# Attention's first batch in two passes over its tiles of queries, with loads and operands in two portions

## The chip, the cores and the metric

The kernel runs on one core of a Trainium2 chip. The metric is the device time of one execution in microseconds (us), the median of several runs. Five engines work side by side, each on its own queue of instructions in program order: TensorE (PE, the matrix engine), VectorE (DVE), ScalarE (ACT), GpSimd (POOL) and SyncE (SP, which here only issues transfers).

## The reference

Attention over 4 batches of 8 heads, 576 positions and head size 64, with a causal mask and a bias from a running sum of gates, feeds a dense mixture of 8 experts:

```python
scores = scale * np.matmul(q, k.transpose(0, 1, 3, 2))
cum = np.cumsum(np.maximum(s, 0.0), axis=-1)
bias = -(cum[:, :, :, None] - cum[:, :, None, :])
scores = np.where(causal, -1000000000.0, scores + np.minimum(bias, 0.0))
attn = softmax(scores)
x = np.matmul(attn, v)          # 2304 tokens of 512 features
P = x @ w_gate                  # exp, then 8 rounds of row and column scaling
out = sum(P[:, e:e+1] * (relu(x @ w1[e]) @ w2[e]) for e in range(8))
```

The expert layer cuts each expert's 1024 hidden features into 4 units of 256, so there are 32 units.

## The kernel before

**Attention.** The 8 heads of a batch are taken as 4 pairs (`g` counts pairs over all batches, 16 in all). A pair has 5 tiles of 128 queries (`i` = 0 to 4; the last has 64 queries of each head). Because of the causal mask, tile `i` has scores of (i + 1) x 128 columns. One slot of the loop is one tile of one pair, and the steps of a slot are staggered over four turns `ti` of the loop: `st0` makes the scores (tile `sc`), their row minimum (L366, into tile `T`) and the exponential; `st1` normalizes; `st2` transposes (tile `tr`, copied to `at` or `al`); `st3` multiplies with the values (tile `pv`) and writes the result, split in a high and a low part, to `xh` and `xl`.

**Operands of a head.** `load_head` fetches the transposed queries and keys of one head, each twice (to the lower and the upper 64 partitions), so 4 transfers of 144 KB a head. `prep_head` makes from them the operands `qa`, `qb`, `ka`, `kb`: high parts on VectorE, low parts on GpSimd (L329, L333; on VectorE for the first two heads), a copy of the high part by a transfer (`qb<-qa`, L327), and the rows of the gates' running sum by two or three small transfers (L314, L317). The raw tiles have two buffers, so the next head's queries and keys are fetched when GpSimd has read those of the head before.

**The expert layer beside attention.** Its first 4 units run on the first tokens while attention runs. `EARLY` lists, for each batch, blocks of tokens; for a block a unit needs `g1_half` (L104), `relu_parts` (L118 on ScalarE, L119 on VectorE) and `g2_chunk` (L137, L147, L149). These steps stand in a queue, `Stream`; `fill` takes steps from it in each turn. A batch's steps enter the queue when its attention is complete: at `ti` 22, 42 and 62 for batches 0 to 2, after attention for the last. A unit's weights are loaded (`w_load_early`) and split (`w_split_early`: L68 on ScalarE, L69 on GpSimd).

**What sets the order.** The program is recorded by these loops; a scheduler then fixes each engine's order before the launch. At run time every engine, and SP's queue of transfers, works strictly in that order and waits on semaphores. All of attention's loads but the first four are issued by SP.

Of the kernel before, what the change touches and what calls it, by code (L numbers as in the profile page):

```python
# [8 lines left out]
F32 = mybir.dt.float32  # L9
F32R = mybir.dt.float32r  # L10
AF = mybir.ActivationFunctionType
ALU = mybir.AluOpType
# [15 lines left out]
    [(0, 256), (256, 256)],  # L28
# [3 lines left out]
]  # L32
TP = 384
# [4 lines left out]
def fused_kernel(ctx: ExitStack, tc: tile.TileContext, qT, kT, v, s, w_gate, wu, out):  # L38
# [121 lines left out]
    class Stream:  # L160
# [4 lines left out]
        def add_visit(self, vi, load, split):  # L165
# [46 lines left out]
    with ExitStack() as actx:  # L212
# [9 lines left out]
        def load_head(h):  # L222
            tag, bufs = ("raw", 2) if h else ("T", 5)
            for which, src in (("q", qT), ("k", kT)):
                raw = apool.tile([P, S], F32, name=f"raw{which}", tag=tag, bufs=bufs)
                eng = nc.scalar if h < 2 and which == "k" else nc.sync
                eng.dma_start(out=raw[:D], in_=src[h])
                eng.dma_start(out=raw[D:], in_=src[h])
                raws[h, which] = raw
# [3 lines left out]
        load_head(0)  # L233
        load_head(1)
# [8 lines left out]
        crow_d = dram.tile([B * H, 6, S], F32, name="crow_d")  # L243
        cum = apool.tile([B * H, S], F32, name="cum", tag="T", bufs=5)
        cr = xl[: B * H, 2:4, :].rearrange("p k n -> p (k n)")
        cr = cr[:, : 6 * S].rearrange("p (r n) -> p r n", n=S)
        nc.gpsimd.memset(cr[:, 0:2, :].bitcast(F32), 1.0)
        nc.gpsimd.memset(cr[:, 4:6, :].bitcast(F32), -1.0)
# [6 lines left out]
        nc.scalar.copy(cr[:, 2, :], cum)  # L255
        gates_done = nc.vector.tensor_tensor(
            out=cr[:, 3, :], in0=cum, in1=cr[:, 2, :].bitcast(F32), op=ALU.subtract
# [25 lines left out]


        QW = S + D
        qas, qbs, vtt = [], [], []
        for n in range(4):
            qa = apool.tile([P, QW], F32R, name=f"qa{n}")
            qb = apool.tile([D + 4, QW], F32R, name=f"qb{n}")
            z = slice(S - D, S) if n % 2 else slice(S, QW)  # L290
            nc.gpsimd.memset(qa[:, z].bitcast(F32), 0.0)
            nc.gpsimd.memset(qb[:, z].bitcast(F32), 0.0)
            qas.append(qa)
            qbs.append(qb)

        for n in range(2):
            vt = apool.tile([P, 5, P], F32, name=f"vt{n}")
            nc.gpsimd.memset(vt[:D, 4, :], 0.0)
            vtt.append(vt)

        ops = {}

        def prep_head(h):
            rq, rk = raws.pop((h, "q")), raws.pop((h, "k"))
            ka = apool.tile([P, S], F32R, name="ka", tag="ka", bufs=4)
            kb = apool.tile([D + 4, S], F32R, name="kb", tag="kb", bufs=4)
            qa, qb = qas[h % 4], qbs[h % 4]
            if h < 2:
                rows = cr[h : h + 1].bitcast(F32)
            else:  # L310
                rows = crow_d[h : h + 1]
            at = [(0, 0, S)] if h % 2 == 0 else [(0, 0, S - D), (S - D, S, D)]
            for i, o, n in at:
                nc.sync.dma_start(  # L314
                    out=qb[D : D + 4, o : o + n].bitcast(F32), in_=rows[:, 2:6, i : i + n]
                )
            nc.sync.dma_start(out=kb[D : D + 4, :].bitcast(F32), in_=rows[:, 0:4, :])  # L317
            for i, o, n in at:
                nc.vector.tensor_scalar(  # L319
                    out=qa[:, o : o + n], in0=rq[:, i : i + n], scalar1=-1.0, scalar2=None,  # L320
# [634 lines left out]
```

## Time and profile before

| what | value |
|---|---|
| median of 3 runs | 1766.21 us (1765.97 to 1766.9) |
| the profiled execution, its own time | 1765.97 us |
| its span, first to last instruction | 1764.2 us (1.8 us lie outside it) |
| TensorE busy | 1724.8 us, 98% of the span |
| VectorE busy | 1185.0 us, 67% |
| ScalarE busy | 597.3 us, 34% |
| GpSimd busy | 461.2 us, 26% |
| mean granted TensorE clock | 0.995 of full speed |

A busy share is an average over the whole program. The first 90 us, attention of batch 0, look unlike the rest: there TensorE has gaps, and from about 95 us to 340 us it has nearly none.

### The profile page before, as it was taken

To read this page: it belongs to the slowest core of one execution; us is meant where nothing else is said; L and a number is where in the kernel's file an instruction comes from. 1 tells how busy PE (TensorE), PEld (TensorE's weight loads), DVE (VectorE), ACT (ScalarE), POOL (GpSimd) and SP (SyncE) were. 2 spreads that over 40 slices of the span, in tenths; PEclk is the share of its full clock that TensorE was granted. 3 is DMA by queue.
4 is the path that set the end of the run, shared out by engine and by line. 5 is a ranking of instruction groups with operands and counts; after the bars stand their busy time and mean duration, and the time that the engine had idled before them with its cause. 6 is when DMAs were issued, how large, how long until landed. Compare 5 with 4: busy or idle time off the path is not lost.

```text
span 1764.2 us, 26154 instructions
## 1 busy us (share of the span) xinstructions
PE 1724.8 (98%) x9629; PEld 1536.3 (87%) x9629; DVE 1185.0 (67%) x2394; ACT 597.3 (34%) x1419; POOL 461.2 (26%) x511
## 2 busy tenths in 40 slices
PE   5799999999999999999999999999999999999999
PEld 4688888878988888888888888888888888888887
DVE  6777676689666666666666666666666666666665
ACT  5776766543422222222222222222222222222221
POOL 4653443123221222221222222221222222222210
PEclk9899999999999999999999999999999999999999
DMA  6543433111000000000000000000000000000002
GB/s 169 160 142 91 126 90 96 44 36 55 13 24 24 14 25 25 25 25 24 25 25 19 24 19 25 25 25 20 17 25 25 25 25 25 25 25 18 23 2 108
DMA packets 44271, 77.26 MB, mean 44 GB/s; under 512 B 5936, under 2 KB 15152, under 8 KB 44112
## 3 DMA queue, kind: packets, MB, share of 16 engines
q1 hardware_dynamic: 43824, 75.00, 14.0%
q8 instruction: 76, 1.25, 0.3%
q10 hardware_dynamic: 320, 0.59, 0.1%
q14 instruction: 51, 0.42, 0.1%
HBM read 65.13 MB, written 5.16 MB: 40 GB/s over the span
## 4 chain that ended last, share of the span: by engine, by line
PE 92%; DVE 4%; DMA 2%; issue 1%; ACT 0%; SPq 0%; POOL 0%; DVEq 0%; POOLq 0%; ACTq 0%
PE g L137 44%; PE c L815 35%; PE g L104 5%; PE sc L357 3%; PE pv L460 2%; PE tr L430 2%; DVE xs L719 1%; DMA rawq<-qT 1%; DMA rawk<-kT 1%; PE g L483 0%; DVE acc L149 0%; DVE xel L719 0%; DVE T L366 0%; DVE hl L119 0%; DVE qa L319 0%
## 5 line engine op out<-in xcount | busy, mean ns | idle before, releaser
L137 PE MATMUL g<-w,hh 128*128 128x512 f32 x2304 | 711.6, 396 | 0.2 <-DVE acc L149 0.2
L153 DVE SCALAR_TENSOR_TENSOR acc<-g,prob,acc 128x512 f32<-128x512 f32 x504 | 377.1, 748 | 236.0 <-PE g L137 234.8
L137 PEld LDWEIGHTS g<-w,hh 128*128 128x128 f32 x2304 | 424.0, 188 | 64.1 <-issue 0.5
L137 PE MATMUL g<-w,hl 128*128 128x512 f32 x1152 | 442.2, 396 | 3.2 <-DVE hl L119 3.2
L118 ACT ACTIVATE hh<-tap 128x384 fp32r<-128x384 f32 x336 | 176.4, 526 | 680.2 <-DVE tap L828 356.2
L815 PE MATMUL c<-xh,wc 128*128 128x384 f32 x1344 | 398.9, 337 | 0.0
L828 DVE TENSOR_TENSOR tap<-c,tap 128x384 f32<-128x384 f32 x588 | 320.2, 557 | 52.9 <-PE c L815 31.8
L119 DVE SCALAR_TENSOR_TENSOR hl<-tap,hh 128x384 fp32r<-128x384 f32 x336 | 189.3, 564 | 170.5 <-ACT hh L118 160.4
L815 PE MATMUL c<-xeh,wc 128*128 128x384 f32 x1008 | 297.8, 335 | 0.0
L137 PEld LDWEIGHTS g<-w,hl 128*128 128x128 f32 x1152 | 216.3, 188 | 55.5 <-DVE hl L119 4.4
L815 PEld LDWEIGHTS c<-xh,wc 128*128 128x128 f32 x1344 | 247.8, 188 | 11.3
L815 PE MATMUL c<-xl,wc 128*128 128x384 f32 x672 | 226.8, 337 | 0.0
L69 POOL TENSOR_TENSOR wc<-r,wc 128x256 fp32r<-128x256 f32 x112 | 85.5, 764 | 465.5 <-ACT wc L68 465.5
L815 PEld LDWEIGHTS c<-xeh,wc 128*128 128x128 f32 x1008 | 187.1, 188 | 11.2
L69 POOL TENSOR_TENSOR w<-r,w 128x512 fp32r<-128x512 f32 x64 | 86.8, 1358 | 391.6 <-ACT w L68 387.9
L815 PE MATMUL c<-xel,wc 128*128 128x384 f32 x504 | 170.6, 338 | 0.0
L815 PEld LDWEIGHTS c<-xl,wc 128*128 128x128 f32 x672 | 125.9, 187 | 11.3
L104 PE MATMUL g<-xh,w 128*128 128x256 f32 (+1 forms) x512 | 115.8, 302 | 1.9 <-DVE hl L119 1.0
L399 ACT ACTIVATE T<-T,mn 128x128 f32<-128x128 f32 (+2 forms) x144 | 83.8, 582 | 66.3 <-DVE mn L366 59.3
L815 PEld LDWEIGHTS c<-xel,wc 128*128 128x128 f32 x504 | 94.5, 188 | 4.0
L68 ACT CAST wc<-r 128x256 fp32r<-128x256 f32 x112 | 45.1, 403 | 147.6 <-PE c L815 147.6
L104 PEld LDWEIGHTS g<-xh,w 128*128 128x128 f32 x512 | 87.2, 192 | 4.8 <-DVE acc L149 1.7
(123 smaller groups left out, 1627.6 us busy)
## 6 DMA issues: line engine op xcount, KB each, us to landing
r<-wu SPq DMA_DIRECT2D x30, 512.0 KB
r<-wu SPq DMA_DIRECT2D x60, 256.0 KB
rawq<-qT SPq DMA_DIRECT2D x64, 144.0 KB
wraw<-wu SPq DMA_DIRECT2D x36, 256.0 KB
rawk<-kT SPq DMA_DIRECT2D x60, 144.0 KB
qb<-qa SPq DMA_DIRECT2D x32, 160.0 KB
out<-acc SPq DMA_DIRECT2D x18, 256.0 KB
vt<-v SPq DMA_DIRECT2D x16, 256.0 KB
```

The source lines that it names most:

```text
L68: nc.scalar.copy(dst, src)
L69: nc.gpsimd.tensor_tensor(out=lo, in0=src, in1=dst.bitcast(F32), op=ALU.subtract)
L104: nc.tensor.matmul(ps[:, :n], lhsT=w1[:, w, o : o + P], rhs=x[:, k, n0 : n0 + n], start=(k == 0 and t == 0), stop=(k == KD - 1 and t == 2),)
L118: nc.scalar.activation(hh[:, :n], src, AF.Relu)
L119: nc.vector.scalar_tensor_tensor(out=hl[:, :n], in0=src, scalar=0.0, in1=hh[:, :n].bitcast(F32), op0=ALU.max, op1=ALU.subtract,)
L137: nc.tensor.matmul(ps, lhsT=h[:, cs], rhs=w2[:, w, f * DM : (f + 1) * DM], start=(f == 0 and t == 0), stop=(f == NFC - 1 and t == 2),)
L153: nc.vector.scalar_tensor_tensor(out=a, in0=ps, scalar=prob[:, c, e : e + 1], in1=a, op0=ALU.mult, op1=ALU.add)
L357: nc.tensor.matmul(out, lhsT=queries(q, h, i), rhs=k[:, cols], start=(first and n == 0), stop=(last and n == 1),)
L399: nc.scalar.activation(T[:, :n], T[:, :n], AF.Exp, bias=mn[:, 1:2], scale=-1.0, accum_out=sums[t][:, j : j + 1],)
L430: nc.tensor.transpose(tr[:, c * P : (c + 1) * P], T[:, c * P : (c + 1) * P], ident)
L815: nc.tensor.matmul(ps[:, :TP], lhsT=w[:, i % 4, wl_, k], rhs=x(xl_, k), start=(k == 0 and t == 0), stop=(k == 1 and t == 2),)
L828: nc.vector.tensor_tensor(out=dst, in0=ps, in1=t, op=ALU.add)
```

## The change

Batch 0 is taken in two passes. The first pass does tiles 0 and 1 of all four pairs (8 slots), the second tiles 2, 3 and 4 of all four pairs (12 slots). The first 256 tokens are then complete at turn 10, and become a block of `EARLY` of their own, whose expert steps enter the queue at turn 10 instead of with the rest at turn 22. A head's queries and keys are loaded in two portions, columns 0 to 255 (64 KB a transfer) and 256 to 575 (80 KB); the first portions of all heads go to tiles of the output accumulator (`acc4` to `acc11`) that are free at that time, and the operands of heads 4 to 7 to parts of `xh` and `xl` that are not yet in use. The values are loaded in two portions as well. The gates' rows of heads 0 to 7 are taken from `xl`, two rows a transfer; the constant rows are set by GpSimd (`blank`). One reload of unit 1 is dropped, and there are 20 visits of units to blocks in place of 16.

```diff
 EARLY = [
-    [(0, 256), (256, 256)],
+    [(0, 256)],
+    [(256, 256)],
     [(512, 256), (768, 384)],
     [(1152, 256), (1408, 256)],
     [(1664, 256), (1920, 384)],
 ]
+C1 = 256
...
-    for b in range(B):
+    for b in range(len(EARLY)):
...
-            if vi + 1 in loads:
+            if vi and vi + 1 in loads:
                 nu = loads[vi + 1]
+                if len(blocks) == 1:
+                    at = len(seq) - 4
...
+        def load_head(h, c0=0, c1=S, scratch=False):
+
+            for n, (which, src) in enumerate((("q", qT), ("k", kT))):
+                if scratch:
+                    raw = acc[4 + h][:, n * (c1 - c0) : (n + 1) * (c1 - c0)]
+                else:
+                    raw = apool.tile([P, S], F32, name=f"raw{which}", tag="raw", bufs=2)
+                    raw = raw[:, : c1 - c0]
+                eng = nc.scalar if h < 2 and c0 == 0 and which == "k" else nc.sync
+                eng.dma_start(out=raw[:D], in_=src[h, :, c0:c1])
+                eng.dma_start(out=raw[D:], in_=src[h, :, c0:c1])
                 raws[h, which] = raw
...
+        def blank(n):
+            qa, qb, ka, kb = opn[n]
+            z = slice(S - D, S) if n % 2 else slice(S, QW)
+            nc.gpsimd.memset(kb[D:].bitcast(F32), 1.0)
+            nc.gpsimd.memset(qb[D:].bitcast(F32), -1.0)
+            nc.gpsimd.memset(qb[:, z].bitcast(F32), 0.0)
+            nc.gpsimd.memset(qa[:, z].bitcast(F32), 0.0)
...
-        def prep_head(h):
+        def prep_head(h, c0=0, c1=S):
             rq, rk = raws.pop((h, "q")), raws.pop((h, "k"))
...
+            if c0 == 0:
+                rows = cr[h : h + 1].bitcast(F32) if h < 8 else crow_d[h : h + 1]
+                for i, o, n in [(0, 0, S)] if h % 2 == 0 else [(0, 0, S - D), (S - D, S, D)]:
+                    nc.sync.dma_start(
+                        out=qb[D : D + 2, o : o + n].bitcast(F32), in_=rows[:, :, i : i + n]
+                    )
+                nc.sync.dma_start(out=kb[D + 2 : D + 4, :].bitcast(F32), in_=rows)
...
-        slots = [(g, i) for g in range(B * NPAIR) for i in range(5)]
+        slots = [(g, i) for g in range(NPAIR) for i in (0, 1)]
+        slots += [(g, i) for g in range(NPAIR) for i in (2, 3, 4)]
+        slots += [(g, i) for g in range(NPAIR, B * NPAIR) for i in range(5)]
...
-        prep_head(0)
-        prep_head(1)
+        prep_head(0, 0, C1)
+        prep_head(1, 0, C1)
+        load_v(0, (0,))
+        for h in (2, 3):
+            load_head(h, 0, C1, True)
         nc.sync.dma_start(out=crow_d, in_=cr.bitcast(F32))
-        load_v(0)
-        load_head(2)
+        blank(2)
+        blank(3)
+        for h in (4, 5):
+            load_head(h, 0, C1, True)
+        load_v(1, (0,))
+        blank(4)
+        blank(5)
+        for h in (6, 7):
+            load_head(h, 0, C1, True)
+        blank(6)
+        blank(7)
+        load_v(2, (0,))
+        load_v(3, (0,))
+        for n in range(4):
+            nc.gpsimd.memset(vtt[n][2][:D, 0], 0.0)
+        load_head(0, C1, S)
         wgr = const.tile([P, KD * 8], F32, name="wgr")
         nc.sync.dma_start(out=wgr, in_=w_gate)
...
-            nxt = min([x for x in (23, 43, 63) if x > ti] + [NS + 3])
+            nxt = min([x for x in (30 if ti < 22 else 43, 43, 63) if x > ti] + [NS + 3])
             budget[0] += len(stream.queue) / (2.0 * (nxt - ti))
...
+            if ti < 6:
+                if i == 0:
+                    prep_head(2 * g + 2, 0, C1)
+                    prep_head(2 * g + 3, 0, C1)
+                else:
+                    load_v(g, (1,))
+            elif ti < 8:
+                prep_head(ti - 6, C1, S)
+                load_head(ti - 5, C1, S)
+                if ti == 7:
+                    load_v(3, (1,))
+            elif ti < NS and g + 1 < NG and i in ((2, 3) if g < NPAIR else (1, 3)):
+                h = 2 * (g + 1) + (i == 3)
+                prep_head(h, C1 if h < 8 else 0)
                 if h + 1 < B * H:
-                    load_head(h + 1)
-            if 4 <= ti < 18:
-                u, r = divmod(ti - 4, 7)
+                    load_head(h + 1, C1 if h + 1 < 8 else 0)
+            if 3 <= ti < 17:
+                u, r = divmod(ti - 3, 7)
...
+            if ti in (10, 22, 42, 62, 82):
+                bb = (10, 22, 42, 62, 82).index(ti)
+                if bb < B:
+                    for k in range(4):
+                        stream.add_visit(4 * bb + k, w_load_early, w_split_early)
...
-    for vi in range(12, 16):
+    for vi in range(16, 20):
         stream.add_visit(vi, load_plain, split_plain)
```

In the new program's names, `acc6` holds the raw queries and keys of head 2, `acc10` of head 6, `acc11` of head 7; `qa2` is an operand of head 2; for heads 4 to 7 operands read as `xh` and `xl`. Line numbers of the changed kernel are some 40 to 70 higher.

**SP, early in the program.** Before, around the loads of heads 2 and 3 (`rawq`, `rawk`: raw queries and keys, `wgr`: the gate's weights, `crow_d`: the gates' rows):

```order
L227 DMA rawq_184<-qT 64x576
L228 DMA rawq_184<-qT 64x576
L227 DMA rawk_187<-kT 64x576
L228 DMA rawk_187<-kT 64x576
L532 DMA wgr_190<-w_gate 128x32
L314 DMA qb2_149<-crow_d_115 4x576
L317 DMA kb_230<-crow_d_115 4x576
L327 DMA qb2_149<-qa2_148 64x640
L227 DMA rawq_238<-qT 64x576
```

After, the end of the row of loads that follows the operands of heads 0 and 1:

```order
L235 DMA acc11_82<-kT 64x256
L236 DMA acc11_82<-kT 64x256
L383 DMA acc2_73<-v 128x2x128
L383 DMA acc3_74<-v 128x2x128
L235 DMA rawq_232<-qT 64x320
L236 DMA rawq_232<-qT 64x320
L235 DMA rawk_235<-kT 64x320
L236 DMA rawk_235<-kT 64x320
L591 DMA wgr_238<-w_gate 128x32
L342 DMA qb2_120<-xl_70 2x1x576
L345 DMA kb2_122<-xl_70 2x1x576
L359 DMA qb2_120<-qa2_119 64x256
```

Before, the small transfers of head 2 stand behind 5 loads that follow the first two heads. Now they stand behind the first portions of all of heads 2 to 7, the values and the second portion of head 0: 33 transfers, the 14th to the 46th.

**VectorE, at the step from pair 0 to pair 1.** Before (`T_368` is the first row minimum of pair 1; `raw` and `_229`, `_304` belong to heads 2 and 3):

```order
L366 ISA T_322,mn_323<-sc_325,mask_123 128x288
L366 ISA mn_323 128x1
L319 TENSOR_SCALAR qa3_152<-rawq_238 128x512
L319 TENSOR_SCALAR qa3_152<-rawq_238 128x64
L366 ISA T_322,mn_323<-sc_331,mask2_132,mn_323 128x288
L366 ISA mn_323 128x1
L418 RECIPROCAL rec_339<-sm_276 128x2
L324 TENSOR_SCALAR ka_304<-rawk_241,sgn_112 128x576
L366 ISA T_368,mn_369<-sc_371,mask_123 128x128
```

After (`T_294` is the first row minimum of pair 1):

```order
L350 TENSOR_SCALAR xl_70<-acc9_80 128x256
L355 TENSOR_SCALAR xh_69<-acc9_80,sgn_108 128x256
L350 TENSOR_SCALAR xl_70<-acc10_81 128x256
L355 TENSOR_SCALAR xh_69<-acc10_81,sgn_108 128x256
L350 TENSOR_SCALAR xl_70<-acc11_82 128x256
L355 TENSOR_SCALAR xh_69<-acc11_82,sgn_108 128x256
L350 TENSOR_SCALAR qa0_111<-rawq_232 128x320
L355 TENSOR_SCALAR ka0_113<-rawk_235,sgn_108 128x320
L593 CAST wg_66<-wgr_238 128x4x8
L594 TENSOR_TENSOR wg_66<-wgr_238,wg_66 128x4x8
L404 ISA T_294,mn_295<-sc_297,mask_141 128x128
```

Before, the operands of one head stand ahead of it among pair 0's last tile. Now the operands of heads 4 to 7, those of head 0's second portion and the gate's weights all stand ahead of it.

**TensorE, in the second pass.** Before, between two tiles of pair 2 (`g` with `xh` or `xl` is a step of the expert layer):

```order
L104 MATMUL g_1234<-xh_69,w1_501 128x256
L483 MATMUL g_1246<-xl_70,wg_66 16x256
L430 MATMUL tr_624<-ident_64,T_508 128x128 x4
L357 MATMUL sc_692<-ka_431,qa0_140 128x384
L357 MATMUL sc_692<-kb_432,qb0_141 128x384
L430 MATMUL tr_631<-ident_64,T_516 128x128 x4
L357 MATMUL sc_699<-ka_538,qa1_144 128x384
L357 MATMUL sc_699<-kb_539,qb1_145 128x384
L357 MATMUL sc_749<-ka_431,qa0_140 128x512
```

After, likewise between the tiles of pairs 1 and 2:

```order
L468 MATMUL tr_874<-ident_64,T_709 128x128 x3
L395 MATMUL sc_895<-xh_69,xl_70 128x384 x2
L395 MATMUL sc_943<-xh_69 128x512 x2
L139 MATMUL g_1110<-w2_607,hh_833 128x512 x2
L139 MATMUL g_1110<-w2_607,hl_834 128x512
L139 MATMUL g_1110<-w2_607,hh_966 128x512 x2
L139 MATMUL g_1110<-w2_607,hl_967 128x512
L139 MATMUL g_1175<-w2_607,hh_833 128x512 x2
L139 MATMUL g_1175<-w2_607,hl_834 128x512
L139 MATMUL g_1175<-w2_607,hh_966 128x512 x2
L139 MATMUL g_1175<-w2_607,hl_967 128x512
L468 MATMUL tr_904<-ident_64,T_752 128x128 x4
```

Single steps of the first unit stood there before; now whole chunks of both matrix products of the first units do.

## Rows read from the trace of the kernel before

**Rows 1.** The page: busy time, share of the span and instructions of TensorE; and TensorE's busy tenths in 40 equal slices of 44.1 us.

```profile
span 1764.2 us, 26154 instructions
PE 1724.8 (98%) x9629; PEld 1536.3 (87%) x9629; DVE 1185.0 (67%) x2394; ACT 597.3 (34%) x1419; POOL 461.2 (26%) x511
...
PE   5799999999999999999999999999999999999999
```

**Rows 2.** Busy time of each engine by stretch: stretch (us), its length, then busy us (instructions) of PE, PE's weight loads, DVE, ACT, POOL, then granted clock, DMA share and GB/s.

```profile
0.00:93.60 93.60, 65.44 (x496) 53.70 (x497) 64.83 (x207) 61.71 (x173) 50.06 (x64) 0.91 0.58 159
...
85.00:90.00 5.00, 5.00 (x24) 4.51 (x24) 2.15 (x8) 2.48 (x7) 3.30 (x4) 0.50 0.73 202
...
140.00:340.00 200.00, 199.67 (x1649) 177.91 (x1649) 141.53 (x434) 134.93 (x372) 69.67 (x56) 1.00 0.33 93
```

**Rows 3.** SP's queue in order of time: start us, us, what it issued.

```profile
1.21 0.55 SPq L227 DMA_DIRECT2D rawq<-qT  x1
1.80 0.59 SPq L228 DMA_DIRECT2D rawq<-qT  x1
...
3.06 0.60 SPq L228 DMA_DIRECT2D rawq<-qT  x1
...
10.38 0.61 SPq L317 DMA_DIRECT2D kb<-xl  x1
11.04 1.19 SPq L314 DMA_DIRECT2D qb<-xl  x2
12.28 0.57 SPq L317 DMA_DIRECT2D kb<-xl  x1
...
13.38 0.55 SPq L350 DMA_DIRECT2D vt<-v  x1
...
18.30 0.29 SPq L317 DMA_DIRECT2D kb<-crow_d  x1
...
29.55 1.06 SPq L515 DMA_DIRECT2D wraw<-wu  x2
```

**Rows 4.** The same start on the other engines, in order of time (in brackets the idle time before and what ended it): when the gates' transfer had landed, the gates' last step, TensorE's first matmul and the second products, which need `qb` and `kb`.

```profile
2.71 0.66 DVE L249 TENSOR_SCALAR s_sb<-s_sb 32x576 f32<-32x576 f32 x1 [2.71 <-DMA s_sb<-s]
...
8.83 0.74 DVE L256 TENSOR_TENSOR xl<-cum,xl 32x576 fp32r<-32x576 f32 x1
...
10.84 0.47 PE L357 MATMUL sc<-ka,qa 128*128 128x128 f32 x1 [10.84 <-DVE qa L333]
...
14.19 0.80 PE L357 MATMUL sc<-kb,qb 68*128 68x128 f32 x2
```

**Rows 5.** DMA queues in the first 30 us: packets, MB, share of 16 engines' time.

```profile
q1 hardware_dynamic: 2997, 3.97, 51.6%
```

**Rows 6.** The chain that ended last, two pieces where TensorE runs without a gap: start us, us, what.

```profile
96.58 1.42 PE g L104 x12
...
447.96 2.79 PE g L137 x12
```

**Rows 7.** VectorE in order of time: row minima that open a pair's first tile (`T` of 128 columns) and third tile (384 columns), and the last step of a pair (`xl`, 320 columns).

```profile
26.61 0.28 DVE L366 CUSTOM_DVE_ANT_0 T<-sc,mask 128x128 f32<-128x128 f32 x1
...
32.38 0.55 DVE L366 CUSTOM_DVE_ANT_0 T<-sc,mask 128x384 f32<-128x384 f32 x1
...
44.40 0.28 DVE L366 CUSTOM_DVE_ANT_0 T<-sc,mask 128x128 f32<-128x128 f32 x1
...
50.36 0.55 DVE L366 CUSTOM_DVE_ANT_0 T<-sc,mask 128x384 f32<-128x384 f32 x1
...
56.40 0.48 DVE L471 TENSOR_TENSOR xl<-pv,xh 128x320 fp32r<-128x320 f32 x1
...
61.62 0.28 DVE L366 CUSTOM_DVE_ANT_0 T<-sc,mask 128x128 f32<-128x128 f32 x1
...
68.85 0.54 DVE L366 CUSTOM_DVE_ANT_0 T<-sc,mask 128x384 f32<-128x384 f32 x1
...
72.84 0.48 DVE L471 TENSOR_TENSOR xl<-pv,xh 128x320 fp32r<-128x320 f32 x1
...
77.43 0.28 DVE L366 CUSTOM_DVE_ANT_0 T<-sc,mask 128x128 f32<-128x128 f32 x1
...
89.46 0.55 DVE L366 CUSTOM_DVE_ANT_0 T<-sc,mask 128x384 f32<-128x384 f32 x1
...
94.04 0.49 DVE L471 TENSOR_TENSOR xl<-pv,xh 128x320 fp32r<-128x320 f32 x1
```

**Rows 8.** Groups of instructions by line, shapes kept apart, from 85 to 260 us: line, engine, operation, count | busy us, mean ns of one | idle before.

```profile
L149 DVE TENSOR_TENSOR acc<-g,acc 128x512 f32<-128x512 f32 x22 | 15.1, 685 | 5.9 <-PE g L137 5.9
L68 ACT CAST w<-wraw 128x512 fp32r<-128x512 f32 x18 | 10.3, 618 | 2.6 <-DMA wraw<-wu 2.0 <-issue 0.6
L119 DVE SCALAR_TENSOR_TENSOR hl<-g,hh 128x256 fp32r<-128x256 f32 x23 | 9.5, 417 | 0.5 <-ACT hh L118 0.2
L118 ACT ACTIVATE hh<-g 128x256 fp32r<-128x256 f32 x23 | 8.6, 374 | 3.8 <-PE g L104 3.7
L147 ACT COPY acc<-g 128x512 f32<-128x512 f32 x9 | 5.2, 574 | 1.9 <-PE g L137 1.9
```

**Rows 9.** Who waited for whom in the first 130 us: engine, line, what it waited for: us in total, times, longest.

```profile
DVE qa L319 <- DMA rawq<-qT: 9.7, 6, 3.2
DVE ka L324 <- DMA rawk<-kT: 5.2, 4, 2.5
```

More of the change, by code (lines that the diff above doesn't have):

```diff
@@ L239, in fused_kernel @@
         nc.gpsimd.memset(sgn[D:], -1.0)
-        crow_d = dram.tile([B * H, 6, S], F32, name="crow_d")
+        QW = S + D
+        opn = []
+        place = lambda x, k, o, n: x[:, k, S + o : S + o + n]
+        kplaces = [place(xh, i // 3, i % 3 * S, S) for i in range(8)]
+        qplaces = [place(xl if i else xh, (3, 0, 1, 2)[i], o, QW) for i in range(4) for o in (0, QW)]
+        for n in range(8):
+            if n < 4:
+                qa = apool.tile([P, QW], F32R, name=f"qa{n}")
+                qb = apool.tile([D + 4, QW], F32R, name=f"qb{n}")
+                ka = apool.tile([P, S], F32R, name=f"ka{n}")
+                kb = apool.tile([D + 4, S], F32R, name=f"kb{n}")
+            else:
+                qa, qb = qplaces[2 * n - 8], qplaces[2 * n - 7][: D + 4]
+                ka, kb = kplaces[2 * n - 8], kplaces[2 * n - 7][: D + 4]
+            opn.append((qa, qb, ka, kb))
+        def blank(n):
[5 more added lines that the diff above has]
+            nc.gpsimd.memset(qa[:, z].bitcast(F32), 0.0)
+        blank(0)
+        blank(1)
+        crow_d = dram.tile([B * H, 2, S], F32, name="crow_d")
         cum = apool.tile([B * H, S], F32, name="cum", tag="T", bufs=5)
[L245 to L248, printed above, removed]
+        cr = xl[: B * H, 3, S : 3 * S].rearrange("p (r n) -> p r n", n=S)
         nc.vector.tensor_scalar(
@@ L296, in fused_kernel @@
-        for n in range(2):
-            vt = apool.tile([P, 5, P], F32, name=f"vt{n}")
-            nc.gpsimd.memset(vt[:D, 4, :], 0.0)
+            if n < 2:
+                vt = apool.tile([P, 5, P], F32, name=f"vt{n}")
+                vt = [vt[:, 0:2], vt[:, 2:4], vt[:, 4:5]]
+            else:
+                vt = [acc[n][:, :256], acc[n][:, 256:], acc[12][:, (n - 2) * P : (n - 1) * P]]
+                vt = [t.rearrange("p (c d) -> p c d", d=P) for t in vt]
             vtt.append(vt)
-        ops = {}
@@ L303, in prep_head @@
-        def prep_head(h):
+        def prep_head(h, c0=0, c1=S):
             rq, rk = raws.pop((h, "q")), raws.pop((h, "k"))
[L305 to L309, printed above, removed]
-            else:
[L311 to L315, printed above, removed]
-                )
[L317 to L320, printed above, removed]
-                    op0=ALU.mult,
-                )
-            with tc.issue_after(gates_done.ins) if h < 2 else ExitStack():
-                nc.vector.tensor_scalar(
-                    out=ka, in0=rk, scalar1=sgn[:, 0:1], scalar2=None, op0=ALU.mult
-                )
-                nc.sync.dma_start(out=qb[:D].bitcast(F32), in_=qa[:D].bitcast(F32))
-                lo = nc.vector if h < 2 else nc.gpsimd
@@ new lines, in prep_head @@
+            first = h < 2 and c0 == 0
+            behind = lambda x: tc.issue_after(gates_done.ins) if x else ExitStack()
+            with behind(first and h == 1):
+                for i, o, n in at:
+                    nc.vector.tensor_scalar(
+                        out=qa[:, o : o + n], in0=rq[:, i - c0 : i - c0 + n], scalar1=-1.0,
+                        scalar2=None, op0=ALU.mult,
+                    )
+            with behind(first):
+                nc.vector.tensor_scalar(
+                    out=ka[:, c0:c1], in0=rk, scalar1=sgn[:, 0:1], scalar2=None, op0=ALU.mult
+                )
+                qc = slice(c0, c1 if c1 < S else QW)
+                nc.sync.dma_start(out=qb[:D, qc].bitcast(F32), in_=qa[:D, qc].bitcast(F32))
+                lo = nc.vector if first else nc.gpsimd
@@ L550, in fused_kernel @@
                 g, i = slots[ti]
-                if i == 3 and g + 1 < NG:
+                if i == 3 and NPAIR <= g + 1 < NG:
                     load_v(g + 1)
@@ L579, in fused_kernel @@
                     w_split_early(u, r - 3)
[L581 to L588 removed]
+            if ti in (10, 22, 42, 62, 82):
[3 more added lines that the diff above has]
+                        stream.add_visit(4 * bb + k, w_load_early, w_split_early)
+                for x, (n0, n) in enumerate(EARLY[bb]):
+                    stream.queue.insert(4 * x + 1, lambda n0=n0, n=n: gate(n0, n))
+                    stream.queue.insert(4 * x + 3, lambda n0=n0, n=n: gate_t(n0, n))
         stream.flush()
```

72 lines of the change are left out of this document (28 added, 44 removed).

## The prediction

> **What bounds the kernel now.** The page comes first: TensorE is busy 98% of the span, and its only slices well below full are the first two, up to 88 us [rows 1]. The table by stretch narrows it down. From 140 to 340 us TensorE is busy 199.67 of 200 us while VectorE has 141.5 and ScalarE 134.9 [rows 2]: there matmuls alone set the pace, and a change of order gains nothing. So the change can only act in the first 90-odd us, where attention of batch 0 has no expert steps beside it. There no engine is full: to 93.6 us VectorE is busy 64.8, ScalarE 61.7, GpSimd 50.1 us [rows 2]; slots are chains between engines, and VectorE also stops for loads, 9.7 and 5.2 us in the first 130 us [rows 9].
>
> TensorE's busy time misleads here, since a lone matmul counts with its latency. I therefore compare the two kernels at a milestone, the last step of batch 0's attention (`xl` of its fourth pair), which stands at 94.04 us [rows 7]. In both orders, TensorE has by the last `pv` of that pair issued the same attention: 110 score matmuls, 101 transposes and 120 products with the values, and the same 14 + 2 matmuls of the gate. The changed one has issued more of the expert layer: 60 in place of 24 of the first product, and 24 in place of none of the second. A gapless run costs 1.42 us for 12 of the first and 2.79 for 12 of the second [rows 6], so the extra is 36 x 0.118 + 24 x 0.2325 = 9.9 us of work that need not be done later. As TensorE is full afterwards, the change pays if the milestone comes before 94.0 + 9.9 = 103.9 us, and costs what it comes later.
>
> **The change part by part: the queue of transfers.** SP issues nearly every load, one after the other. Four loads of 144 KB start from 1.21 to 3.06 us, 0.62 us apart; a load of 32 KB takes 0.55 us to issue, operand rows from `xl` 0.57 to 0.61, two weight pieces of 256 KB 1.06 together, rows from DRAM 0.29 [rows 3]. So size hardly matters, and I take 0.62 us for a load of 64 KB, which the trace does not show (ends: 0.29 and 0.65). The new order has 46 transfers before the first operand rows of head 2. The four query loads start as before, but the fourth waits for the semaphore of an earlier transfer, to about 4.1 us. The gates' transfer lands 2.0 us after its issue at 0.74 (2.71) [rows 4], and the halves are smaller, so heads 0 and 1 start earlier: the first matmul near 7 us in place of 10.84, the operand rows of head 1 issued by 10 us. Then 33 loads at 0.62 us take 20.5, to 30.4 us; three transfers at 0.6 for head 2, landing 1.9 us after their start (from 12.28 to the matmul at 14.19 [rows 3, 4]). The first row minimum of pair 1 is thus at 33.9 us; before it was at 26.61, with three more tiles of pair 0 done [rows 7]. VectorE gives the same time: ahead of this row minimum it has the gate's weights, the 46th transfer, which land at about 32.4 us.
>
> Bytes are not the limit: 3.97 MB took 51.6% of 16 engines in 30 us, 62 ps a byte and engine [rows 5], so 64 KB need 0.25 us of all 16, less than the 0.62 of their issue.
>
> A rule of the Trainium skill speaks against the change here (DMA: Bandwidth & Descriptors, Rules for kernel authors): many small transfers should be merged, since under 64 KB one pays mostly overhead. The issue times above agree with it, down to 32 KB. If issue instead went with bytes, 64 KB would cost 0.28 us and the 33 loads 9 us in place of 20.5; that is the first rival.
>
> **The first pass.** After 33.9 us three pairs are left. Two short tiles took 5.8, 6.0 and 7.2 us of a pair before (26.61 to 32.38, 44.40 to 50.36, 61.62 to 68.85) [rows 7]; three times their mean, 6.3, ends the first pass at 52.9. SP agrees: behind head 2's rows stand 24 more transfers to the last operand of head 7, 14.4 us, so that one starts at 46.0 and lands at 47.9, and its pair's tiles follow. I put the first row minimum of the second pass at 52.5 us (48 if issue took 0.5 us, 54 at the most). Until then TensorE has had little to do: the first expert product needs all four pairs and starts no earlier.
>
> **The second pass.** Before, the three long tiles took 12.0, 11.2 and 8.6 us of pairs 1 to 3 (32.38 to 44.40, 50.36 to 61.62, 68.85 to 77.43) [rows 7]. Four pairs at 10.5 us make 42 us (34 to 48). The new work beside them: VectorE has 3 more `hl` at 0.417 and 2 accumulations at 0.685, ScalarE 3 more `hh` at 0.374, 2 copies at 0.574 and 4 weight pieces at 0.618 [rows 8], 2.6 and 4.7 us; the high parts come in two instructions, about 1.3 us more on VectorE. In chains without much slack I take 5 us (0 to 8). From the first tile of the next pair to a pair's last `xl` it was 12.0 and 11.2 us (44.40 to 56.40, 61.62 to 72.84) [rows 7]; I take 11.5. The milestone: 52.5 + 42 + 5 + 11.5 = 111.0 us, which is 7.1 us after 103.9.
>
> **What costs nothing.** The memsets of `blank` stand on GpSimd ahead of head 2's low parts; whatever they take is hidden until head 2's rows arrive at 33.5 us. The one unit more of weights lies beside full TensorE from 140 us on, where ScalarE has 65 us of 200 to spare and GpSimd 130 [rows 2]; without that cover it would be 4 pieces, some 5 us. The dropped reload was waited for nowhere. Batch 1 has 9.9 us less expert work beside it, so TensorE may run dry there; VectorE is busy 71% in that stretch [rows 2], and I take 0 (up to 4 us).
>
> **Sum.** 1765.97 us of the profiled execution + 7.1 = 1773.1 us. Its time is 0.24 us below the median of the runs shown, which I neglect.
>
> **The rivals.**
> - *Issue gets cheap* (faster). If a transfer of 64 KB or of two rows costs some 0.3 us, SP reaches the end of the first pass's operands near 30 us, and the first pass, then bound by its tiles, starts at 24 and ends at 24 + 19 = 43 us; the raw loads of 80 KB then also arrive in time, and the long tiles go at 8.6 us. Milestone 43 + 34.4 + 5 + 11.5 = 93.9, 10 us before par: 1756 us. For it speaks 0.29 us for rows from DRAM; against it every load of queries and keys [rows 3]. It decides where the second pass begins before 45 us.
> - *The second pass runs smoothly* (no change). The load waits of VectorE [rows 9] shrink with 320 columns in place of 576, and all pairs go at 8.6 us: 52.5 + 34.4 + 5 + 11.5 = 103.4, 0.5 us before par: 1765.5 us. Against it: the second pass has SP issue 66 transfers more, 40 us by itself.
> - *Expert steps in the way* (much slower). Before, the first two tiles of pair 4 took 12.0 us (77.43 to 89.46) in place of 6.3 [rows 7]: a run of expert matmuls stood ahead of them on TensorE, at a granted clock of 0.50 (1.2 GHz) from 85 to 90 us [rows 2], after a stretch with gaps. If each pair of the second pass loses half of those 5.7 us, four lose 11.4: 1784.5 us.
>
> The Trainium skill states for that clock (TensorE: Matmul & The Clock Gate, HAM oscillation) that gaps on TensorE bring the lower clock back. If fuller work kept it high, the 2.5 us that these 5 us cost would come back; I count them as equal in both.
>
> **How the numbers follow.** My forecast (the sum, alone 1768 to 1781 us) has 0.50, expert steps in the way 0.15: both slower. The smooth second pass has 0.15, cheap issue 0.20. Differences within 0.2%, 3.5 us, are about what a measurement of this kernel cannot tell from no change. So faster 0.20, same 0.15, slower 0.65. The range from 1757 to 1787 us reaches from just inside the first rival to just past the last one, and leaves 1 in 10 on either side.
>
> **What would show it.** In the changed trace: the 46th transfer of SP issued near 30 us; VectorE idle from about 15 to 32 us, in waits for loads; the first row minimum of pair 1 near 34 us, that of pair 0's third tile near 52; batch 0's last `xl` near 111; TensorE without gaps from there. The prediction is wrong if SP issues these loads much faster than 0.6 us apart, or if the long tiles take well under 10 us a pair with the expert steps among them.

## The result

The changed kernel takes 1792.17 us (median of 4 runs, 1791.07 to 1792.79) against 1766.55 us of the kernel before beside it: a ratio of 1.0145, with a 95% interval from 1.0132 to 1.0157. It is 25.6 us slower. The prediction, 1773.1 us in a range from 1757 to 1787, had the direction and 7 of the 26 us.

### The profile page after: what moved, and what is told of

Its sections match the earlier page's. It is cut to its first block, busy times and chain, and to the rows that moved or that the text cites. A ratio compares the mean times of both kernels' runs of the same rounds, so it can differ in the third digit from the quotient of the medians.

```text
span 1789.9 us, 26305 instructions
## 1 busy us (share of the span) xinstructions
PE 1733.6 (97%) x9629; PEld 1539.1 (86%) x9629; DVE 1184.5 (66%) x2409; ACT 598.4 (33%) x1423; POOL 479.9 (27%) x556
## 4 chain that ended last, share of the span: by engine, by line
PE 88%; DVE 5%; DMA 3%; SPq 2%; POOL 1%; ACT 1%; issue 1%; DVEq 0%; POOLq 0%; ACTq 0%
PE g L139 43%; PE c L885 34%; PE g L106 4%; PE pv L498 2%; PE sc L395 2%; PE tr L468 2%; DVE xs L789 1%; DMA rawq<-qT 1%; DMA wraw<-wu 1%; DMA rawk<-kT 1%; SPq L235 1%; DVE at L473 0%; DVE T L404 0%; SPq L236 0%; DVE acc L151 0%
## 5 line engine op out<-in xcount | busy, mean ns | idle before, releaser
L885 PEld LDWEIGHTS c<-xeh,wc 128*128 128x128 f32 x1008 | 187.1, 188 | 11.2
L437 ACT ACTIVATE T<-T,mn 128x128 f32<-128x128 f32 (+4 forms) x144 | 83.7, 582 | 78.3 <-DVE mn L404 70.3
L106 PEld LDWEIGHTS g<-xh,w 128*128 128x128 f32 x512 | 87.2, 191 | 7.0 <-DVE acc L151 1.7
```

The lines of the kernel that those rows point to most:

```text
L106: nc.tensor.matmul(ps[:, :n], lhsT=w1[:, w, o : o + P], rhs=x[:, k, n0 : n0 + n], start=(k == 0 and t == 0), stop=(k == KD - 1 and t == 2),)
L437: nc.scalar.activation(T[:, :n], T[:, :n], AF.Exp, bias=mn[:, 1:2], scale=-1.0, accum_out=sums[t][:, j : j + 1],)
L885: nc.tensor.matmul(ps[:, :TP], lhsT=w[:, i % 4, wl_, k], rhs=x(xl_, k), start=(k == 0 and t == 0), stop=(k == 1 and t == 2),)
```

## The profile after

The page of the changed kernel, the same rows as in [rows 1]: span, busy time by engine, TensorE's busy tenths in 40 slices.

```profile
span 1789.9 us, 26305 instructions
PE 1733.6 (97%) x9629; PEld 1539.1 (86%) x9629; DVE 1184.5 (66%) x2409; ACT 598.4 (33%) x1423; POOL 479.9 (27%) x556
...
PE   3899999999999999999999999999999999999999
```

TensorE has as many matmuls as before. The loss again lies in the first slices. SP's queue in order of time (answers to [rows 3]):

```profile
1.21 0.56 SPq L235 DMA_DIRECT2D acc<-qT  x1
...
10.27 0.59 SPq L235 DMA_DIRECT2D acc<-qT  x1
10.90 0.59 SPq L236 DMA_DIRECT2D acc<-qT  x1
...
30.21 0.58 SPq L591 DMA_DIRECT2D wgr<-w_gate  x1
...
32.29 0.53 SPq L359 DMA_DIRECT2D qb<-qa  x1
...
47.70 0.52 SPq L359 DMA_DIRECT2D xl<-xl  x1
```

The 33 transfers from the 14th on start 0.62 us apart, though most of them carry 64 KB; the 46th transfer is issued at 30.21 us, the last operand of the first pass at 47.70. VectorE in order of time (answers to [rows 7]): the first row minimum of pair 1, the first of 384 columns of each of the four pairs, the first of the next batch, and the last `xl` of the batch, the milestone:

```profile
35.01 0.29 DVE L404 CUSTOM_DVE_ANT_0 T<-sc,mask 128x128 f32<-128x128 f32 x1 [1.67 <-PE sc L395]
...
54.93 0.55 DVE L404 CUSTOM_DVE_ANT_0 T<-sc,mask 128x384 f32<-128x384 f32 x1
...
64.88 0.55 DVE L404 CUSTOM_DVE_ANT_0 T<-sc,mask 128x384 f32<-128x384 f32 x1
...
83.23 0.54 DVE L404 CUSTOM_DVE_ANT_0 T<-sc,mask 128x384 f32<-128x384 f32 x1
...
95.34 0.55 DVE L404 CUSTOM_DVE_ANT_0 T<-sc,mask 128x384 f32<-128x384 f32 x1
...
109.44 0.28 DVE L404 CUSTOM_DVE_ANT_0 T<-sc,mask 128x128 f32<-128x128 f32 x1
...
122.08 0.48 DVE L509 TENSOR_TENSOR xl<-pv,xh 128x320 fp32r<-128x320 f32 x1
```

The second pass lasts 54.5 us (54.93 to 109.44); its pairs take 9.95 (the first expectation below has 12.1 for it), 18.35, 12.1 and 14.1 us. The pair of 18.35 us shows how. TensorE's two score matmuls of head 4 (operands in `xh`), and VectorE around the row minimum that waits for them:

```profile
75.73 0.34 PE L395 MATMUL sc<-xh 128*128 128x384 f32 x1
...
76.14 0.34 PE L395 MATMUL sc<-xh 68*128 68x384 f32 x1
```

```profile
76.93 1.11 DVE L350 TENSOR_SCALAR xl<-rawq 128x256 fp32r<-128x256 f32 x2 [1.57 <-DMA rawq<-qT]
...
82.46 0.33 DVE L350 TENSOR_SCALAR xl<-rawq 128x320 fp32r<-128x320 f32 x1 [1.24 <-DMA rawq<-qT]
82.70 0.15 DVE L456 RECIPROCAL rec<-sm 128x1 f32<-128x1 f32 x1
82.78 0.54 DVE L473 COPY at<-tr 128x384 f32<-128x384 f32 x1
83.23 0.54 DVE L404 CUSTOM_DVE_ANT_0 T<-sc,mask 128x384 f32<-128x384 f32 x1
```

The scores are there at 76.5, their row minimum runs 6.7 us later: ahead of it in VectorE's order stand the operands of heads 5 and 6, and these wait for their raw queries. Why those come late is in the chain that ended last (start us, us, what):

```profile
67.92 2.82 DMA rawq<-qT
70.75 1.17 DVE xh L350
...
72.05 0.88 POOL xh L366
...
74.09 2.75 DMA rawq<-qT
...
76.93 1.12 DVE xl L350 x2
78.07 1.02 POOL xl L366 x2
...
79.86 2.50 DMA rawq<-qT
```

A load, VectorE's high part, GpSimd's low part, then the next head's load: a loop of 5.8 to 6.2 us a head here, which the heads of all four pairs go through. Last, busy time by stretch of the changed kernel from 140 to 210 us, where the attention of batch 1 is, in the columns of [rows 2]:

```profile
140.00:210.00 70.00, 66.28 (x548) 56.10 (x547) 51.43 (x162) 49.51 (x138) 31.67 (x25) 0.98 0.41 113
```

Before, TensorE was busy 199.67 of the 200 us from 140 on [rows 2].

**The account.** "Par" is the milestone of before, 94.04 us, corrected for the expert matmuls that a kernel has issued by its own milestone, counted in each trace, at the prediction's 0.118 and 0.2325 us. After has 60 and 24 of them, as predicted, so par is 103.9. "Slower" is the median less that of the runs of before beside it; what is left after "behind par" was lost behind the milestone. Median and milestone come from different executions, so this last column is good to some 3 or 4 us: with the profiled executions' own times, against 1765.97 us, it reads 7.4 for after, 5.1 with the steps spread, 8.0 for the cut block and 7.1 with its casts on GpSimd.

| kernel | long tiles from, to | second pass | milestone | par | behind par | slower | lost behind it |
|---|---|---|---|---|---|---|---|
| predicted | 52.5, 99.5 | 47 | 111.0 | 103.9 | 7.1 | 7.1 | 0 |
| after | 54.9, 109.4 | 54.5 | 122.1 | 103.9 | 18.2 | 25.6 | 7.4 |
| after, merged loads | 42.2, 97.7 | 55.5 | 111.1 | 103.9 | 7.2 | 10.0 | 2.8 |
| after, late steps | 55.0, 104.8 | 49.7 | 114.6 | 92.6 | 22.0 | 28.5 | 6.5 |
| after, ring | 54.6, 108.3 | 53.7 | 119.6 | 103.9 | 15.7 | 22.3 | 6.6 |
| after, two heads ahead | 56.1, 100.4 | 44.3 | 113.0 | 103.9 | 9.1 | 13.2 | 4.1 |
| after, weights at once | 54.0, 107.4 | 53.4 | 119.0 | 103.9 | 15.1 | 21.5 | 6.4 |
| after, casts on GpSimd | 54.7, 107.7 | 53.0 | 118.2 | 103.9 | 14.3 | 19.3 | 5.0 |
| after, steps spread | 55.2, 108.5 | 53.4 | 118.8 | 99.7 | 19.1 | 20.6 | 1.5 |
| after, ahead, weights, spread | 58.4, 103.3 | 45.0 | 114.2 | 99.7 | 14.5 | 16.9 | 2.4 |
| after, ahead, weights, merged | 44.9, 94.6 | 49.7 | 105.9 | 103.9 | 2.0 | 6.0 | 4.0 |
| after, all four | 44.5, 92.7 | 48.3 | 101.1 | 99.7 | 1.4 | 4.0 | 2.6 |
| before, cut block | | | 91.4 | 92.6 | -1.2 | 4.2 | 5.4 |
| before, cut block, casts on GpSimd | | | 87.2 | 92.6 | -5.4 | 1.6 | 7.0 |

Busy time from the milestone to 460 us, before and then in the changed kernel, and two stretches of the latter (columns of [rows 2]):

```profile
94.04:460.00 365.96, 358.64 (x2706) 317.67 (x2704) 273.88 (x783) 223.04 (x591) 124.00 (x101) 1.00 0.28 81
```

```profile
122.08:460.00 337.92, 326.98 (x2513) 286.25 (x2512) 249.59 (x740) 203.95 (x557) 119.72 (x97) 0.99 0.30 85
...
190.00:195.00 5.00, 2.84 (x19) 2.19 (x19) 3.62 (x15) 4.50 (x17) 2.60 (x2) 1.00 0.44 125
195.00:200.00 5.00, 5.00 (x20) 3.37 (x19) 2.09 (x8) 2.66 (x9) 1.72 (x3) 0.66 0.56 148
```

TensorE is idle 10.9 us there, before 7.3: 3.6 of the 7.4 us. Some 1.7 more, an estimate, are the clock, 0.66 over the 5 us from 195 on, which follow 5 us with TensorE idle for 2.2. Where the other 2.1 us went is open.

## The experiments

**Merged loads.** The host lays queries and keys out twice, so that a load of both halves of the partitions is one transfer of the same bytes. In the changed kernel, and in the kernel before:

```diff
-                eng.dma_start(out=raw[:D], in_=src[h, :, c0:c1])
-                eng.dma_start(out=raw[D:], in_=src[h, :, c0:c1])
+                eng.dma_start(out=raw, in_=src[h, :, c0:c1])
```

> The changed kernel, but the host lays queries and keys out twice, so that each load of queries or keys is one transfer to 128 partitions in place of two to 64: same bytes, half the issues. If the issue of transfers by SP holds the first pass, 16 of the first 46 transfers fall away, pair 1 starts some 10 us earlier (25 in place of 35 us), the second pass near 45 in place of 55, and the time falls by about 10 us to 1782. If the bytes or the engines held it, nothing moves: 1792.

> The kernel before, with queries and keys laid out twice by the host and loaded by one transfer each. If VectorE's 15 us of waits for loads there came from their issue, batch 0's attention ends 4 to 8 us earlier: 1758 to 1762 us. If issue plays no part in the kernel before: 1766.

The changed kernel falls to 1776.25 us (1.0057 of before, 1.0041 to 1.0074), 15.6 us less, each beside its own runs of before. In the first pass SP now issues a whole load in 0.43 to 0.58 us, and the gate's weights start at 18.82 in place of 30.21. SP's queue of the changed kernel with merged loads, then VectorE's row minima in it (the first of pair 1, the first of 384 columns, the first of the next batch):

```profile
11.56 0.44 SPq L235 DMA_DIRECT2D acc<-kT  x1
...
18.82 0.43 SPq L590 DMA_DIRECT2D wgr<-w_gate  x1
```

```profile
23.78 0.28 DVE L403 CUSTOM_DVE_ANT_0 T<-sc,mask 128x128 f32<-128x128 f32 x1
...
42.18 0.56 DVE L403 CUSTOM_DVE_ANT_0 T<-sc,mask 128x384 f32<-128x384 f32 x1 [1.50 <-ACT sm L451]
...
97.72 0.27 DVE L403 CUSTOM_DVE_ANT_0 T<-sc,mask 128x128 f32<-128x128 f32 x1
```

The first pass ends 12.7 us sooner, and the second is as long as it was, 55.5 us. So the count of transfers on SP holds the first pass, as the prediction said, and not the second. The Trainium skill says of two transfers to the two halves of the partitions that one of 128 partitions should be used (DMA: Bandwidth & Descriptors, Rules for kernel authors); here that is worth 15.6 us. In the kernel before the same edit gives only 2.1 us, 1764.14 us (0.9989, 0.998 to 0.9998).

**Late steps.** The first block's expert steps enter the queue at turn 22 in place of 10. The time is that of a first run, the rows in the account those of a second, a single execution.

```diff
-            if ti in (10, 22, 42, 62, 82):
-                bb = (10, 22, 42, 62, 82).index(ti)
+            for bb in {22: (0, 1), 42: (2,), 62: (3,), 82: (4,)}.get(ti, ()):
```

> The changed kernel, but the expert steps of the first 256 tokens enter the queue at turn 22 with the others, so no expert matmul stands in the second pass. If expert steps in the way of the tiles made the second pass slow (12.1, 18.4, 12.1 and 14.1 us from one pair's third tile to the next), it falls to some 10.5 us a pair, batch 0's attention ends 12 us or more earlier, more than the 9.9 us of work put off, and the time falls to 1785 us or less. If the steps only fill gaps that something else makes (transfers), attention ends at most a few us earlier and the work comes later: 1795 to 1802 us.

> The same program as the run with the first block's steps at turn 22, for its trace. If the expert steps stretch the second pass (the prediction put them at 5 us), its second pass is about 50 us in place of 54.5. If the loads and the engines' order do, it stays at 53 to 56 us.

1796.27 us (1.0166, 1.0149 to 1.0183), and 1795.95 in the second run: 3 to 4 us slower than the changed kernel. The second pass is 4.8 us shorter, but 72 matmuls that stood in its gaps, 11.2 us by the prices above, are done later. The steps do stretch the second pass by the 5 us that the prediction took, and are still worth having there.

**Ring, and two heads ahead.** The raw second portions go to tiles of the accumulator, four heads deep; then also each is fetched two heads ahead.

```diff
+                elif h < 8:
+                    raw = acc[4 + 2 * (h % 4) + n][:, : c1 - c0]
...
-                load_head(ti - 5, C1, S)
+                load_head(ti - 4, C1, S)
...
-                if h + 1 < B * H:
-                    load_head(h + 1, C1 if h + 1 < 8 else 0)
+                if h < 6:
+                    load_head(h + 2, C1)
+                elif 7 <= h < B * H - 1:
+                    load_head(h + 1)
```

(The load of head 1's second portion then stands at turn 5.)

> The changed kernel, but the raw second portions of heads 0 to 7 go to the eight free accumulator tiles in turn, so four heads can be in flight in place of one. If the loop over the one pair of raw buffers (load, high part on VectorE, low part on GpSimd, next load; 5.8 us a head in the trace) holds the second pass, its four pairs take some 42 us in place of 54.5 and the time falls by about 12 us to 1780. If VectorE, ScalarE or expert steps hold it, it moves by less than 3 us: 1789 to 1792.

> The changed kernel, with the second portions of the raw queries and keys in a ring of four heads (as in the run with the ring), and each fetched two heads ahead instead of one: so SP issues a head's loads before it waits for the head in front of it. Theory A (in the second pass each head's loads are released by the operands of the head before, a loop of 5.8 us a head over SP, VectorE and GpSimd, and this loop makes the second pass 54.5 us): the second pass (first long tile of pair 1 of the batch to the first tile of the next batch) falls from 54.5 to about 46 us, the time to about 1783 us. Rival B (the loop is only one of several chains of the same length, weights and in-order engines being the others): the second pass stays over 52 us, the time at 1786 to 1790 us.

The ring alone: 1788.57 us (1.013, 1.0115 to 1.0145), a second pass of 53.7 us. More buffers do little, because SP issues the next head's loads behind the copy `qb<-qa` of the head in front. With the loads ahead of that copy: 1780.62 us (1.0076, 1.0061 to 1.0091), and the second pass takes 44.3 us, with the same expert steps in it. SP's queue of that run; the four loads of head 5 now stand ahead of the copy of head 4 (`xh<-xh`), where the changed kernel issues them behind it:

```profile
65.27 0.59 SPq L237 DMA_DIRECT2D acc<-qT  x1
65.96 0.54 SPq L238 DMA_DIRECT2D acc<-qT  x1
66.60 0.54 SPq L237 DMA_DIRECT2D acc<-kT  x1
67.19 0.59 SPq L238 DMA_DIRECT2D acc<-kT  x1
67.87 1.22 SPq L555 DMA_DIRECT2D wraw<-wu  x2
69.18 0.49 SPq L361 DMA_DIRECT2D xh<-xh  x1
```

So the loop of loads made the second pass long, 10.2 of its 54.5 us, of which more buffers alone give back 0.8.

**Weights at once; casts on GpSimd.** The first two units' four pieces are fetched together into free accumulator tiles; in another run the high parts of the weights beside attention are cast by GpSimd.

```diff
-                    w_load_early(u)
+                    for pc in range(4):
+                        nc.sync.dma_start(out=acc[4 + pc], in_=wu[u, :, pc * 512 : (pc + 1) * 512])
...
-                    w_split_early(u, r - 3)
+                    split_piece(u, r - 3, acc[4 + r - 3])
```

```diff
-            split_piece(u, pc, wraw.pop(pc))
+            split_piece(u, pc, wraw.pop(pc), nc.gpsimd.tensor_copy)
```

> The changed kernel, with the four weight pieces of each of the first two units fetched at once into tiles of the output accumulator that are free then, in place of two buffers that take turns; ScalarE then finds them landed. Theory C (ScalarE and GpSimd stand still in program order for weight pieces, 7.5 us of ScalarE's waits between 54 and 110 us, and hold the tiles behind them): second pass some 6 us shorter, about 1785 us. Rival (those waits lie beside the loop of raw loads and cost nothing by themselves): within 2 us of the changed kernel's 1792.

> The changed kernel with the casts on GpSimd, loads as they were. If ScalarE's waits for weight pieces (7.5 us between 54 and 110 us) hold the second pass: 1784 to 1787 us; if GpSimd's low parts, which then stand behind these waits, are what matters: 1792 us or more.

1788.92 us (1.0123, 1.0108 to 1.0138) and 1785.94 us (1.0111, 1.0097 to 1.0124): 4.1 and 6.3 us less than the changed kernel, each beside its own runs of before (the interval of the first overlaps the changed kernel's). The second time is the one expected if ScalarE's waits held the second pass. But with the casts on GpSimd the 7.5 us of these waits are gone, and the second pass shrinks by 1.5 us only, with the weights at once by 1.1. So they are a smaller cost of the order, not the reason for the second pass.

**Steps spread.** The first block's steps are spread to turn 43 in place of 30.

```diff
-            nxt = min([x for x in (30 if ti < 22 else 43, 43, 63) if x > ti] + [NS + 3])
+            nxt = min([x for x in (43, 63) if x > ti] + [NS + 3])
```

> The changed kernel, with the first block's expert steps spread to turn 43 instead of turn 30 (a share of 12/33 in place of 12/20 before turn 22, so more steps are left for the next batch). Theory D (about 7 us are lost between 140 and 210 us because too few expert steps are left to fill TensorE beside batch 1): TensorE is busy over 69 of 70 us from 140 to 210 us in place of 66.3, and the time falls by about 3 us, to 1789. Rival E (the gaps there come from something else, such as weights or short visits of units): no change, or as in the run with the late steps some 4 us slower.

1788.00 us (1.0114, 1.0097 to 1.0131), and more of the steps are left for batch 1 (busy time by stretch):

```profile
140.00:210.00 70.00, 68.21 (x582) 59.25 (x581) 50.82 (x165) 49.94 (x142) 31.45 (x25) 1.00 0.41 116
```

TensorE is busy 68.2 of these 70 us in place of 66.3, short of the 69 expected. The time falls by 4.2 us, 5.0 with each beside its own runs of before; the two intervals just part. How much of that lies behind the milestone is less clear than the 1.5 in place of 7.4 us of the account: the profiled execution took 1790.18 us, and by its own time 5.1 us are lost there. From the milestone to 460 us its TensorE is idle 10.5 us, hardly less than the 10.9 of the changed kernel, because gaps of 1.5 us now stand ahead of 140 us:

```profile
118.79:460.00 341.21, 330.71 (x2543) 289.95 (x2542) 252.80 (x747) 206.31 (x562) 123.63 (x101) 1.00 0.30 88
```

What is missing there is the stretch at the lower clock. So the edit pays, but that batch 1 ran dry of steps, which the prediction had named and taken nothing for, is shown only in part.

**The cut block alone.** The kernel before with `[(0, 256)], [(256, 256)]` for the first batch, both entering at turn 22; attention unchanged. Then the same with the casts on GpSimd.

> The kernel before, with only the first batch's block of 512 tokens cut into two blocks of 256 (20 visits of units to blocks in place of 16, both blocks' steps entering at turn 22, the first reload of unit 1 dropped); attention's order and loads stay. The prediction costed this part at nothing. If that holds: 1766 us, within 2 us of before. Rival (visits of half the tokens need each unit's weights twice as often, and the waits between the two products of a short visit show on TensorE in batch 1's stretch, where the changed kernel lost about 4 us between 140 and 210 us): 1769 to 1772 us, with TensorE busy 66 to 68 of these 70 us.

> The kernel before with the cut block (the run that gave 1770.3 us) and, beside attention, the high parts of the weight pieces cast by GpSimd in place of ScalarE. Theory F (a short visit's second product waits for hl behind ScalarE's casts and their loads; ScalarE is what the more frequent weight pieces hold up): the time falls back to 1766 to 1768 us. Rival G (the waits at the short visits come from the shape itself: the second product has only two chunks of the visit before to run while the first one's relu is made): 1769 to 1771 us, as without the casts moved.

1770.33 us (1.0024, 1.0014 to 1.0034): an edit that the prediction took for free costs 4.2 us. One place in the trace of the first, on TensorE, and then ScalarE just ahead of it:

```profile
102.22 1.22 PE L138 MATMUL g<-w,hh 128*128 128x512 f32 x2 [2.08 <-DVE hl L120]
```

```profile
98.91 0.62 ACT L69 CAST w<-wraw 128x512 fp32r<-128x512 f32 x1
100.06 0.62 ACT L69 CAST w<-wraw 128x512 fp32r<-128x512 f32 x1 [0.53 <-DMA wraw<-wu]
...
101.45 0.36 ACT L119 ACTIVATE hh<-g 128x256 fp32r<-128x256 f32 x1
```

Here a short visit's second product waits 2.08 us for `hl`, whose `hh` stands behind two casts of weights and the wait for one of them. But VectorE, which makes `hl`, was not free earlier either:

```profile
101.30 0.53 DVE L322 TENSOR_SCALAR qa<-rawq 128x512 fp32r<-128x512 f32 x2 [2.97 <-DMA rawk<-kT]
101.75 0.42 DVE L120 SCALAR_TENSOR_TENSOR hl<-g,hh 128x256 fp32r<-128x256 f32 x1
```

It stood 2.97 us at a raw load of the next head, and `hl` follows that head's operand at once; `hh` is ready at about the same time. The chain that ended last runs over that load, 3.74 us, which SP had issued behind two weight pieces. With the casts moved it is 1768.24 us (1.001, 1.0 to 1.0019), 2.6 us less with each beside its own runs of before, though the two intervals overlap, and TensorE is busy 20.00 in place of 17.76 us from 90 to 110. Whether that gap was the casts' or the load's is not shown, since the edit moves both. The account shows that attention itself also ends 4.2 us sooner then, and that 7.0 us are still lost behind it. Of these some 2.5, an estimate, are a stretch that has changed sides: the clock is 0.50 from 90 to 95 us, behind the milestone of 87.2, where before it was 0.50 from 85 to 90 [rows 2], ahead of it. What a cut block costs behind the milestone stays open.

**Together.** Loads ahead, weights at once and steps spread; loads ahead, weights at once and merged; these with the steps spread; and the kernel before with merged loads and the casts moved. In the first three the ring has three heads, since the weights take four of its tiles.

> The changed kernel with three of the cures together: second portions fetched two heads ahead (a ring of three heads here), the first two units' weights fetched at once, the first block's steps spread to turn 43. Apart they gave 11.5, 3.2 and 4.2 us. If they touch different time: 1792 - 19 = 1773 us, still slower than before, since the first pass is still held by SP's queue. If they overlap in the second pass: 1777 to 1781 us.

> The changed kernel with the loads two heads ahead, the weights at once, and each load of queries or keys as one transfer of 128 partitions in place of two (16 us apart from the others). If merging and fetching ahead touch different time (first pass, second pass): 1792 - 16 - 11.5 - 3.2 = 1761 us, a little faster than before. If merging had already taken part of the second pass's loop: 1766 to 1770 us.

> The kernel of the run before this one with the first block's steps spread to turn 43 as well. If the spread still pays as it did alone: 4 us less than that run, about 1757 us. If fewer steps in the second pass only leave TensorE emptier there: equal within 1.5 us.

> The kernel before with merged loads (1764.1 us) and the casts on GpSimd. ScalarE is busy 62 of the first 94 us and waits for weight pieces; if its order holds tiles there, some 2 us less, 1762 us. If GpSimd, which needs another 1 us or so for each of 8 pieces there, delays the low parts instead: 1764 to 1768 us.

1783.02 us (1.0099, 1.0084 to 1.0114), 1772.12 (1.0036, 1.0023 to 1.0049), 1770.14 (1.0023, 1.0012 to 1.0035) and 1765.64 (0.9992, 0.9982 to 1.0002). The gains do not add up: the first two runs are slower than either of their expectations. In the second the long tiles run from 44.9 to 94.6 us, 49.7 in place of 44.3. One cost shows in its trace: four weight pieces of 256 KB are issued right ahead of a raw load of 160 KB (SP's queue), which then takes 5.87 us (its chain that ended last); a load of the same size, behind one piece, takes 3.03 us in the run with merged loads alone (last line):

```profile
50.47 1.81 SPq L653 DMA_DIRECT2D acc<-wu  x4
...
52.93 0.54 SPq L237 DMA_DIRECT2D rawq<-qT  x1
```

```profile
52.93 5.87 DMA rawq<-qT
```

```profile
74.81 3.03 DMA rawk<-kT
```

With all of it the milestone is at 101.1, 1.4 us behind its par of 99.7: attention in two passes then costs about nothing, and gains nothing, and 2.6 us are lost behind it. No version in two passes beat the kernel before; merged loads in the old order are the best that ran.

## Why the prediction was wrong, step by step

- **SP's queue: right.** The 46th transfer is issued at 30.21 us (30.4 said), the first row minimum of pair 1 runs at 35.01 (33.9), the first long tile at 54.93 (52.5). A detail was wrong: the fourth query load did not wait (issued at 3.08, not 4.1). VectorE is idle 10.3 of the 17 us from 15 to 32, as said, but only 5.0 of them in waits for loads. The run with merged loads shows the cause by taking it away.
- **The second pass: the term that failed.** Its 47 us were 54.5. Of the two parts the expert steps were right (5 us said, 4.8 by the late steps). The 42 us were four pairs at the pace of before; without the steps the pass still takes 49.7 us, and with the loads ahead 44.3, steps included, less than the 47. What the prediction missed is that a head's loads wait for the operands of the head in front, and that VectorE holds finished scores behind the next heads' operands. It counted SP's 66 transfers there, 40 us, as work and not as a chain with waits in it. The waits for loads of [rows 9] had shown the pattern.
- **The tail:** 12.6 us, 11.5 said.
- **What costs nothing: the second failure.** Behind the milestone 7.4 us were lost where 0 was taken (up to 4): 3.6 of them idle time of TensorE, some 1.7 a stretch at the lower clock. The kernel before with the cut block alone loses 5.4 to 8.0 there, and is 4.2 us slower in all. Spreading the steps gives 4.2 us, but its trace shows TensorE hardly less idle behind the milestone. Why a cut block costs this is not settled.
- **The sum of the misses:** 2.4 + 7.5 + 1.1 to the milestone and 7.4 behind it, 18.4 us, on 7.1 make 25.5 of the 25.6. The par of 103.9 was right: its terms give 9.8, not 9.9 us, and the products with the values are 240 matmuls in either trace, not 120, which changes nothing between the two.
- **The rivals.** Issue does not get cheap. Its price was wrong too: with the first pass over at 42.2 us, before the 43 that it assumed, the milestone is at 111.1 and not 93.9: the long tiles did not get faster with it. The smooth second pass was near only with loads ahead. Expert steps in the way had the closest time, 1784.5, but not the cause: without the steps the kernel is slower.
- **The clock.** In the changed kernel the mean granted clock was 0.53 from 65 to 70 us, 0.63 from 105 to 110 and 0.66 from 195 to 200, each time in part at the lower level of 1.2 GHz; TensorE had been busy 2.9, 3.2 and 2.8 of the 5 us ahead of each. Before it was 0.50 from 85 to 90 [rows 2]. The prediction counted the cost as equal in both, but the third stretch lies behind the milestone, where the kernel before has none. Nor was TensorE without gaps there, as the prediction had said it would be.

## What to carry to other kernels

Where loads of one head are issued behind copies of the operands of the head in front, cost them as a loop (landing, high part, low part, next load) and not as so many issues: here 5.8 to 6.2 us a head, against 2.5 of issue. Count transfers before bytes, and join the two halves of a load before reordering anything. A block cut in two is not free because the matmuls are the same: look at what each short visit waits for, and at how much filling work the next stage is left with, where the total of that edit, 4 us, is shown and its place is not.

## What the runs showed of the hardware

A load to 128 partitions was issued in about the time of one to 64 (0.43 to 0.58 us, against mostly 0.59 in the changed kernel), with twice the bytes. And a raw load of 160 KB took 5.87 us to land when 1 MB of weights had been issued just ahead of it, in place of 3.03 behind a quarter of that. By the prediction's 62 ps a byte and engine, the weights and the load need some 4.7 us of all 16 engines (an estimate): there the bytes, which the prediction could leave aside for 64 KB loads, count.
